# Sliding-window attention with sinks and a two-layer MLP on one core: a new block order, combined score products, and written lists in place of a planner

## The chip, the cores and the metric

The kernel runs on one core of one Trainium2 chip. The metric is the time in device microseconds (us) of one execution; lower is better. A core has TensorE (PE, matmuls), VectorE (DVE), ScalarE (ACT), GpSimd (POOL) and SyncE (SP). Each engine takes its instructions strictly in the order in which they stand in its queue, and waits at an instruction whose semaphores are not yet reached. POOL and SP also issue DMA transfers, from their own queues.

## The reference

```python
# q, k, v: (4 sequences, 8 heads, 768 tokens, 64), float32; n_sink = 4, window = 128
scores = q @ k.T / 8
keep = (key < 4) | ((query - key >= 0) & (query - key < 128))
a = softmax(where(keep, scores, -1e9))
x = (a @ v) as (3072 tokens, 512)
h = x @ w_in                                   # (512, 2048)
out = (h / (1 + exp(-1.702 * h))) @ w_out      # (2048, 512)
```

Attention has a window of 128 tokens and four sink keys, so a block of 128 queries needs the keys and values of its own block, of the block before it in its sequence (masked to the complementary triangle), and four sink keys. The first block of a sequence needs only itself.

## The kernel before

The 3072 tokens are 24 blocks of 128, six to a sequence: blocks 0, 6, 12 and 18 are first blocks. Two neighbouring blocks make a group (12 groups) for the two-layer product.

For one block the steps are these. Three loads, q, k and v, are issued on POOL (L316, L312), which cast from float32 to float16; they are 128 KB each at the destination. q and k are transposed into `qkT`, for the early blocks by TensorE (L410) with a copy out of PSUM, for the others by a DMA transpose on SP (L429). TensorE makes the scores of eight heads against the own block (`own`) and against the previous block (`prv`), eight matmuls of 128 columns with 64 rows each (L460), and the sinks' scores (`snk`, L483). VectorE merges: `prv` is copied over `own` where the key position lies later than the query (L501), the row maximum follows (L513, L529, L532) and is subtracted into `e` (L568, L583). ScalarE takes the exponential into `a` (L600); for half of the heads of the first four blocks it reads PSUM directly with the maximum as bias (L554). `a` is transposed into `at`, by TensorE for the first four blocks (L636), by a DMA transpose on SP for the others (L668). On POOL two selects then split the merged block: `atp` keeps the previous block's triangle (L603), `at` the own one (L607). TensorE sums the values (`av`: L687 the sinks, L693 own, L697 previous), VectorE divides (`xn`, L708, L709), and `xn` is transposed into `xT`, by TensorE (L722) or by DMA (L733).

For one group, TensorE makes the hidden rows `hT` in eight units of eight matmuls of 256 columns (L754; group 0 in units of one block), ScalarE applies the gate into `gT` (L784; group 0 by tanh, L768 and L775), and TensorE makes the output `o` in four quarters per block (L800), which is copied and stored. All `hT`, `o` and transposes share three PSUM buffers (`mm`); scores have `own` 2 and `pv` 2 (shared by `prv` and `av`), sinks 1. The exponential and the gate need different function tables on ScalarE; a change is one ACT_TABLE_LOAD. The weights come as eight loads of 512 KB on POOL (L325, L334).

The order is made by a planner (class Plan): each step is an Op with a cost, an engine, dependencies and a key out of the list KEYS; the planner plays them against the clock and emits them, and emission stands under `with tc.manual_schedule()`, so that each engine's queue has exactly that order. Loads of the later blocks are spread by due times (`after0`, `after`).

Of the kernel before, what the change touches and what calls it, by code (L numbers as in the profile page):

```python
# [20 lines left out]
D = 64  # L21
D1 = D + 1
NBLK = 24
NG = 12
NEG = -1.0e30
PE, ACT, DVE, POOL, SP = "PE", "ACT", "DVE", "POOL", "SP"
CFG = dict(
    tq=(0, 1, 2, 3, 4, 5, 6, 7),
    ta=(0, 1, 2, 3),
    tx=(0, 1, 2, 3),  # L30
    nb={0: 1, 1: 1, 2: 1, 3: 1},
    wide=(1, 3),
    split=(0,),
    gbatch={},
    tanh=(0,),
    after0=25.0,
    vsb=15.0,
    after=8.0,
    loads="q0 k0 q1 k1 v0 v1 i0 i1 q2 k2 q3 k3 i2 i3 v2 v3 q4 k4 q5 k5 o0 o1 o2 o3 v4 v5".split(),
)  # L40
RING = dict(qkn=4, qkt=8, e32=4, a16=4, at=4, atp=4, xn=3, xt=4, gt=3, osb=4, mm=3, own=2, pv=2, mi=1, th=2)

KEYS = [
    int(x)
    for x in """
# [33 lines left out]
""".split()  # L81
]
# [3 lines left out]
class Buf:  # L86


    def __init__(self, ring, make):
        self.ring, self.make, self.ap, self.left, self.taken = ring, make, None, 0, False  # L90
# [7 lines left out]
class Op:  # L98
    def __init__(self, eng, key, cost, emit, deps=(), take=(), give=(), table=None, lat=0.2, xfer=0.0, after=0.0, batch=0, xt=False):
        self.eng = eng if isinstance(eng, dict) else {eng: cost}  # L100
        self.key, self.emit = key, emit
        self.deps = [d for d in deps if d is not None]
        self.take, self.give, self.table, self.batch = list(take), list(give), table, batch
        self.lat, self.xfer, self.after, self.xt = lat, xfer, after, xt
        self.on = self.start = None
        self.end = self.done = 1.0e9
        for b in self.give:
            b.left += 1

    def need(self):  # L110
        rings = [b.ring for b in self.take if not b.taken]
        return {r: rings.count(r) for r in rings}


class Plan:
    TABLE, LANES = 1.35, 8
    ENGINES = (PE, ACT, DVE, POOL, SP)

    def __init__(self, rings):
        self.ops, self.free, self.blk = [], dict(rings), 0  # L120

    def add(self, *a, **kw):
        op = Op(*a, **kw)
        op.seq, op.blk = len(self.ops), self.blk
        self.ops.append(op)
        return op

    def run(self):
        inf = 1.0e9
        t_eng = {e: 1.0 for e in self.ENGINES}  # L130
        free, table, batch, now = dict(self.free), "exp", 0, 0.0
        order, gives, events = [], [], [1.0]
        pending = {e: sorted((o for o in self.ops if e in o.eng), key=lambda o: (o.key, o.seq)) for e in self.ENGINES}
        events += [op.after for op in self.ops if op.after > 0.0]
        queue = {POOL: [], SP: []}
        lanes = {POOL: [], SP: []}
        count = len(self.ops)

        def finish(op):
            events.append(op.done)  # L140
            for b in op.give:
                b.left -= 1
                b.t = max(getattr(b, "t", 0.0), op.done)
                if b.left == 0:
                    gives.append((b.t, b.ring))
                    events.append(b.t)

        while count or any(queue.values()):
            for item in [x for x in gives if x[0] <= now]:
                gives.remove(item)  # L150
                free[item[1]] += 1
            for e in self.ENGINES:
                if t_eng[e] > now:
                    continue
                for op in pending[e]:
                    if op.start is not None or op.after > now:
                        continue
                    if batch and op.table is not None and op.table != table:
                        continue
                    if any((d.end + 0.03 if d.on == e and not d.xfer else d.done) > now for d in op.deps):  # L160
                        continue
                    if any(free[r] < n for r, n in op.need().items()):
                        continue
# [6 lines left out]
                if op.table is not None:  # L170
                    if op.table != table:
                        cost, table = cost + self.TABLE, op.table
                    if op.table == "gate":
                        batch = (batch or op.batch) - 1
# [688 lines left out]
```

## Time and profile before

| | |
|---|---|
| time, median of 3 runs | 251.15 us (249.34 to 252.67) |
| span of the profiled execution | 249.6 us, 5368 instructions |
| loads on POOL | 72 of 128 KB, some 0.90 us each to issue; 8 of 512 KB, 0.78 us |
| DMA transposes on SP | at 20 (3.4 us to landing), xT 20 (2.5), qkT 16 (4.2) |
| selects of a whole block on POOL | L603 1.10 us, L607 1.11 us |
| selects of half a block | 0.65 us, 0.64 us |
| table loads on ScalarE | 20, 1.283 us each |
| HBM | read 27.43 MB, written 6.29 MB |

Times are from one profiled execution. Busy times are shares of its span; TensorE's matmuls overlap, so the mean time of one is longer than the step from one to the next, which the chain of waits shows. A line of the chain in order of time gives start, length and what ran or was waited for. A timeline gives start, length, engine, line and operation, and in brackets the idle time before it and what ended it. "SPq" and "POOLq" are the engines' queues.

### The profile page before, as it was taken

The page shows a single profiled execution, that of the slowest core. Times are in us where ns is not written, and L with a number is a line of the kernel's source. Part 1 is how long each engine was busy: PE and PEld are TensorE (multiplying, and loading weights), DVE is VectorE, ACT ScalarE, POOL GpSimd, SP SyncE. Part 2 cuts the span into 40 slices and gives each one's busy share as a digit, 9 for nine tenths or more (in the row PEclk, how much of TensorE's full clock was granted, in tenths as well). Part 3 has the DMA queues.
Part 4 walks back from the last instruction along what each step waited for, and adds up shares of the span by engine and source line. Part 5 has one row for each costly group of instructions (what it writes and reads, how often), then busy time and mean ns, then how long its engine had stood idle before and what let it go on. Part 6 is the DMA issues. An engine that isn't in the chain of part 4 may idle for free.

```text
span 249.6 us, 5368 instructions
## 1 busy us (share of the span) xinstructions
PE 222.8 (89%) x2163; PEld 151.4 (61%) x2163; DVE 137.0 (55%) x337; ACT 133.2 (53%) x201; POOL 115.5 (46%) x131
## 2 busy tenths in 40 slices
PE   1649768999949999999979999999999999999993
PEld 0328666567526658648637658667567577585751
DVE  4377978958704659869743855616828826001000
ACT  2363657274733747547564557565474677461521
POOL 8869845872931529229705908474042070300000
PEclk9999979999997999999999999999999999999999
DMA  8999999999999979999999999979980360511202
GB/s 64 150 172 181 182 187 197 137 113 167 150 145 231 97 121 185 138 168 153 163 132 243 97 176 193 96 145 188 146 175 11 65 158 3 131 45 21 84 3 84
DMA packets 134440, 33.05 MB, mean 132 GB/s; under 512 B 127216, under 2 KB 131344, under 8 KB 134416
## 3 DMA queue, kind: packets, MB, share of 16 engines
q0 software_dynamic: 79104, 13.64, 77.4%
q1 hardware_dynamic: 55312, 19.08, 41.2%
q8 instruction: 17, 0.28, 0.5%
q14 instruction: 7, 0.06, 0.1%
HBM read 27.43 MB, written 6.29 MB: 135 GB/s over the span
## 4 chain that ended last, share of the span: by engine, by line
PE 69%; DMA 11%; DVE 8%; POOL 7%; issue 3%; ACT 1%; ACTq 0%; POOLq 0%
PE hT L754 31%; PE o L800 26%; DMA xT<-xn 7%; DMA v<-in_v_dram 4%; POOL qkn L316 3%; PE own L460 3%; PE prv L460 2%; PE av L693 2%; PE av L697 2%; POOL at L607 1%; POOL atp L603 1%; DVE mx L513 1%; PE av L687 1%; POOL v L312 1%; DVE gT L775 1%
## 5 line engine op out<-in xcount | busy, mean ns | idle before, releaser
L754 PE MATMUL hT<-xT,w_in 128*128 128x256 f16 (+1 forms) x832 | 93.7, 269 | 7.7 <-DMA xT<-xn 5.9
L800 PE MATMUL o<-w_out,gT 128*128 128x512 f16 x384 | 91.4, 381 | 0.0
L754 PEld LDWEIGHTS <-w_in 128*128 128x128 f16 x832 | 76.3, 100 | 21.2 <-DMA xT<-xn 6.2
L784 ACT ACTIVATE gT<-hT 128x512 f16<-128x512 f32 x88 | 51.7, 597 | 40.1 <-PE hT L754 39.8
L603 POOL TENSOR_SCALAR_AFFINE_SELECT atp<-at 128x1024 f16<-128x1024 f16 (+1 forms) x23 | 22.5, 978 | 92.7 <-DMA at<-a 89.6
L800 PEld LDWEIGHTS <-gT 128*128 128x128 f16 x384 | 34.8, 98 | 35.3 <-issue 0.7
L501 DVE COPY_PREDICATED own<-later,prv 128x512 f32<-128x512 uint16 x40 | 26.1, 695 | 50.6 <-PE prv L460 45.0
L600 ACT ACTIVATE a<-e 128x1056 f16<-128x1056 f32 (+3 forms) x27 | 24.3, 915 | 21.2 <-issue 15.2
L513 DVE TENSOR_REDUCE mx<-own 128x4 f32<-128x512 f32 x48 | 31.7, 683 | 5.0 <-PE own L460 5.0
L568 DVE TENSOR_TENSOR e<-own,mx 128x512 f32<-128x512 f32 x44 | 29.6, 684 | 1.5 <-DVE mx L532 0.5
L389 ACT COPY osb<-o 128x512 f32<-128x512 f32 x20 | 11.7, 586 | 25.1 <-PE o L800 21.3
L607 POOL TENSOR_SCALAR_AFFINE_SELECT at<-at 128x1024 f16<-128x1024 f16 (+1 forms) x23 | 22.8, 990 | 1.6
L316 POOL DMA_DIRECT2D qkn<-in_k_dram x24 | 21.7, 908 | 3.6 <-DMA w_out<-in_moe_w_out_dram 2.5
L316 POOL DMA_DIRECT2D qkn<-in_q_dram x24 | 21.6, 901 | 2.4 <-DMA w_in<-in_moe_w_in_dram 2.2
L312 POOL DMA_DIRECT2D v<-in_v_dram x24 | 21.7, 907 | 1.9 <-DMA w_in<-in_moe_w_in_dram 1.2
L709 DVE TENSOR_TENSOR xn<-av,rcp 128x256 f16<-128x256 f32 x48 | 20.4, 424 | 1.7
L708 DVE RECIPROCAL rcp<-av 128x4 f32<-128x4 f32 x48 | 8.4, 175 | 20.7 <-PE av L697 19.2
L693 PE MATMUL av<-v,at 128*128 128x65 f16 x192 | 17.5, 196 | 1.0 <-POOL at L607 0.6
L693 PEld LDWEIGHTS <-at 128*128 128x128 f16 x192 | 14.8, 99 | 5.3 <-POOL at L607 1.4
L460 PEld LDWEIGHTS <-qkT 64*128 64x128 f16 x352 | 10.9, 99 | 9.5 <-issue 7.9
L697 PE MATMUL av<-v,atp 128*128 128x65 f16 x160 | 15.0, 193 | 0.0
L410 PE MATMUL tq<-ident,qkn 128*128 128x128 f16 x64 | 7.6, 261 | 7.9 <-DMA qkn<-in_k_dram 5.2
(48 smaller groups left out, 162.6 us busy)
## 6 DMA issues: line engine op xcount, KB each, us to landing
out_dram<-osb SPq DMA_DIRECT2D x24, 256.0 KB, 2.4
qkn<-in_k_dram POOLq DMA_DIRECT2D x24, 128.0 KB, 7.1
qkn<-in_q_dram POOLq DMA_DIRECT2D x24, 128.0 KB, 6.2
v<-in_v_dram POOLq DMA_DIRECT2D x24, 128.0 KB, 7.2
w_in<-in_moe_w_in_dram POOLq DMA_DIRECT2D x4, 512.0 KB, 9.2
w_out<-in_moe_w_out_dram POOLq DMA_DIRECT2D x4, 512.0 KB, 12.0
at<-a SPq DMA_TRANSPOSE x20, 3.4
xT<-xn SPq DMA_TRANSPOSE x20, 2.5
```

The costliest lines, as they stand in the source:

```text
L312: return sw(key, 0.88, lambda: nc.gpsimd.dma_start(v65[:, b, :, 0:D], src), 0.85, deps=[z_1], after=after)
L316: key, 0.88, lambda: nc.gpsimd.dma_start(buf()[:, i, w], src), 0.87,
L501: nc.vector.copy_predicated(out=own[l](), mask=later.unsqueeze(1).to_broadcast((P, 4, P)), data=prv[l]())
L513: lambda l=l, own=own, small=small: nc.vector.tensor_reduce(out=small[:, l], in_=own[l](), axis=AX.X, op=ALU.max),
L568: nc.vector.tensor_tensor(out=e32()[:, 512 * l : 512 * l + 512].rearrange("p (j s) -> p j s", j=4), in0=own[l](), in1=small[:, l].unsqueez ...
L600: nc.scalar.activation(out=a16()[:, lo:hi], in_=e32()[:, lo:hi], func=AF.Exp, scale=scale)
L603: nc.gpsimd.affine_select(out=atp()[:, lo : lo + n], in_=at()[:, lo : lo + n], pattern=[[0, n], [-1, P]], compare_op=ALU.is_gt, fill=0.0, ...
L607: nc.gpsimd.affine_select(out=at()[:, lo : lo + n], in_=at()[:, lo : lo + n], pattern=[[0, n], [1, P]], compare_op=ALU.is_ge, fill=0.0, ba ...
L693: nc.tensor.matmul(av()[:, j], at()[:, c], v65[:, b, h], start=(r == 0), stop=(r == 0))
L754: nc.tensor.matmul(ht()[:, n], w_in16[:, c, bass.ts(f, P)], xt[g]()[:, c, tok], start=(c == 0), stop=(c == 3))
L784: lambda fs=fs, tok=tok, gt=gt, ht=ht: nc.scalar.activation(out=gt()[:, fs[0] : fs[-1] + 1, tok], in_=ht(), func=AF.Gelu_apprx_sigmoid),
L800: nc.tensor.matmul(po(), gt()[:, F, bass.ts(t, P)], w_out16[:, F], start=(F == 0), stop=(F == NF - 1))
```

## The change

The steps of the computation stay, with these differences.

- Blocks run in the order 0, 6, 12, 18, then 1 to 5, 7 to 11, 13 to 17, 19 to 23. Groups are [0], [6], [12, 18], and then two blocks each in that order: [1, 2], [3, 4], [5, 7] and so on.
- `qkT` is one tile of 14 slots, so that the keys of a block and of the one before it can be addressed together by a step. Eight matmuls of 256 columns make both key blocks' scores; the result holds own and previous columns side by side in `sc` (two halves of heads, two PSUM banks each). The merge copies one side over the other.
- The four first blocks read PSUM for all heads in the exponential. Sinks are copied out of PSUM before use, and share one PSUM buffer (`av`, 1) with the values. `mm` stays at three.
- TensorE transposes q and k, and x, for the first eight blocks of the order, and `a` for the first six; the later q/k and x transposes are DMA transposes of two blocks at once.
- A block's loads depend, in the list, on the last select of the block five places earlier.
- The planner and KEYS are gone; ORDER lists the operations, and `Plan.emit` follows it. The emission does not stand under `tc.manual_schedule()`.

```diff
+BLOCKS = [0, 6, 12, 18] + [6 * s + r for s in range(4) for r in range(1, 6)]
+SLOT = {b: (b // 6 if b % 6 == 0 else 4 + 5 * (b // 6 % 2) + b % 6 - 1) for b in range(NBLK)}
+GROUPS = [[0], [6]] + [[12, 18]] + [BLOCKS[n : n + 2] for n in range(4, 24, 2)]
-RING = dict(qkn=4, qkt=8, e32=4, a16=4, at=4, atp=4, xn=3, xt=4, gt=3, osb=4, mm=3, own=2, pv=2, mi=1, th=2)
+RING = dict(qkn=4, qkn2=3, e32=3, a16=4, at=4, atp=3, ss=3, xn=3, xt=4, gt1=2, gt2=2, osb=4, mm=3, sc=2, av=1, th=2)
...
+    def emit(self, order):
+        letter = {"d": DVE, "a": ACT, "p": POOL}
+        seen = set()
+        for word in order.split():
+            choice = letter.get(word[-1])
+            op = self.ops[int(word[:-1] if choice else word)]
+            assert all(d.seq in seen for d in op.deps), op.name
+            seen.add(op.seq)
+            op.emit(choice) if len(op.eng) > 1 else op.emit()
...
+                            nc.tensor.matmul(
+                                t()[:, l, jj], qkT[rows, s, j], qkT[rows, lo : hi + 1 : hi - lo, 4 + j],
+                                start=True, stop=True,
+                            )
...
+                    nc.vector.copy_predicated(
+                        out=t()[:, :, :, own].rearrange("p l j s -> p (l j) s"),
+                        mask=later.unsqueeze(1).to_broadcast((P, 4, P)),
+                        data=t()[:, :, :, 1 - own].rearrange("p l j s -> p (l j) s"),
+                    )
...
+            o = plan.add(f"snk{b}", PE, 0.16, sinks, deps=o_qkt[b] + [o_ks[bb]], take=[snk], key=K0 - 32)
...
+    for pos, b in enumerate(BLOCKS):
+        if pos - AHEAD >= 0 and last_sel.get(BLOCKS[pos - AHEAD]):
+            for w in "qkv":
+                ld[w, b].deps.append(last_sel[BLOCKS[pos - AHEAD]])
...
-    order = plan.run()
-    with tc.manual_schedule():
-        for op in order:
-            op.emit(op.on) if len(op.eng) > 1 else op.emit()
+    plan.emit(ORDER)
```

The dependencies given to `plan.add` are not waits of the program: `emit` only asserts that the list respects them. The waits of the program come from the tiles that an instruction reads and writes.

The list and the built program differ. This is POOL's queue from the start, with the selects named by their block (sp makes `atp`, so makes `at`; halves in the first two blocks) and the number of loads between them:

```
list:   35 loads | sp1 sp1 so1 so1 | 3 | sp2 so2 sp2 so2 | 2 | sp3 | 1 | so3 | 3 | sp4 so4 | 3 | sp5 so5 | 3 | sp7 so7 | ...
built:  48 loads | sp1 sp1 so1 so1 | 7 | sp2 | 1 | so2 | 1 | sp2 | 1 | so2 | 1 | sp3 | 1 | so3 sp4 | 1 | so4 | 10 | sp5 | 1 | so5 | 8 | sp7 so7 sp9 so9 ...
```

Both have eight weight loads among the first. In the built program the 51st load waits, beside its place among the loads in flight, for the DMA transpose of blocks 7 and 8, whose buffer it overwrites. SP's queue in the built program has the DMA transposes in the order qkT of 5, of 7 and 8, of 11, of 9 and 10, at of 3, of 4, qkT of 13 and 14, of 15 and 16, of 17, at of 5, of 7, of 9, xT of 5 and 7, with stores between them. In TensorE's queue av of block 1 stands within the first product of [12, 18], av of block 2 within the second product of [12, 18], av of block 5 between two quarters of the second product of [1, 2], after the first unit of [3, 4], and av of block 7 between quarters of the second product of [3, 4]. ScalarE's queue has 44 table loads (in the list 42).

More of the change, by code (lines that the diff above doesn't have):

```diff
@@ L98, with __init__ @@
 class Op:
-    def __init__(self, eng, key, cost, emit, deps=(), take=(), give=(), table=None, lat=0.2, xfer=0.0, after=0.0, batch=0, xt=False):
+    def __init__(self, name, eng, cost, emit, deps=(), take=(), give=(), table=None, dma=None, key=0.0):
+        self.name, self.emit, self.table, self.dma, self.key = name, emit, table, dma, key
         self.eng = eng if isinstance(eng, dict) else {eng: cost}
-        self.key, self.emit = key, emit
         self.deps = [d for d in deps if d is not None]
[L103 to L108, printed above, removed]
@@ L110, in need, with __init__ @@
-    def need(self):
-        rings = [b.ring for b in self.take if not b.taken]
-        return {r: rings.count(r) for r in rings}
+        self.take, self.give = list(take), list(give)
 class Plan:
[L116 to L120, printed above, removed]
+    def __init__(self):
+        self.ops = []
     def add(self, *a, **kw):
         op = Op(*a, **kw)
-        op.seq, op.blk = len(self.ops), self.blk
+        op.seq = len(self.ops)
@@ new lines, with vs_build @@
+    o_vsb = []
+    for bb in range(Bsz):
+        o = plan.add(
+            f"vsa{bb}", SP, 0.75, lambda bb=bb: nc.sync.dma_start(vsa[:, bb, 0:D], v[bb, :, 0:4, :]),
+            deps=[z_s], dma=("c", 0.3), key=-500 + bb,
+        )
+        def vs_build(e, bb=bb):
+            (nc.vector if e == DVE else nc.gpsimd).tensor_tensor(
+                out=vsb[:, bb].rearrange("p l (j d) -> p (l j) d", d=D1),
+                in0=vsa[:, bb].unsqueeze(1).to_broadcast((32, 8, D1)),
+                in1=ownm.rearrange("p (n d) -> p n d", d=D1),
+                op=ALU.mult,
+            )
+        o_vsb.append(plan.add(f"vsb{bb}", {DVE: 0.6, POOL: 1.15}, 0, vs_build, deps=[o, o_own], key=20))
@@ new lines, with head @@
+    o_qkt, o_ks, o_x = {}, {}, {}
+    xts, used_a16, used_slot, last_sel = {}, {}, {}, {}
+    for grp in GROUPS:
+        t = sb("xt", (P, max(map(len, GROUPS)), 4, P), FP16, f"xT{grp[0]}")
+        for n, b in enumerate(grp):
+            xts[b] = (t, n)
+    def head(i):
+        return 2 * (2 * (i // 4) + i % 2) + i // 2 % 2
+    for pos, b in enumerate(BLOCKS):
+        bb, r = divmod(b, 6)
+        K0 = 10 * pos
+        early = pos < COLD
+        lo, hi = sorted((SLOT[b], SLOT[b - 1])) if r else (0, 0)
+        own = int(r == 0 or SLOT[b] > SLOT[b - 1])
+        qkb = qkT[:, SLOT[b]]
+        buf, n, unit = tunit[b]
+        if b in TQ:
@@ L414 @@
                 a = plan.add(
[L415 to L416 removed]
+                    f"t{'qk'[w]}{b}", PE, 0.43 if early else 0.24, t_qk, deps=[ld["qk"[w], b], o_ident],
+                    take=[tp], give=[buf], key=K0 - 40,
                 )
@@ L439, in sink_keys @@
                     nc.vector.tensor_copy(
-                        out=ksb[rows, bb, :, 4 * hl : 4 * hl + 4], in_=qkt[b]()[rows, 4:8, 0:4]
+                        out=ksb[rows, bb, :, 4 * hl : 4 * hl + 4], in_=qkb[rows, 4:8, 0:4]
                     )
-            o_ks[bb] = plan.add(DVE, K0 - 40, 0.7, sink_keys, deps=o_qkt[b] + [z_k])
-        own = [ps("mm" if b in CFG["wide"] else "own", (P, 4, P), FP32, f"own{b}_{l}") for l in range(2)]
-        prv = [ps("pv", (P, 4, P), FP32, f"prv{b}_{l}") for l in range(2)]
@@ L508 @@
-        mx = []
-        for l in range(2):
-            mx.append(
-                plan.add(
-                    DVE, K0 - 38.9, 0.6,
-                    lambda l=l, own=own, small=small: nc.vector.tensor_reduce(
-                        out=small[:, l], in_=own[l](), axis=AX.X, op=ALU.max
-                    ),
-                    deps=[packs[l]],
+            o_ks[bb] = plan.add(f"ks{b}", DVE, 0.35, sink_keys, deps=o_qkt[b] + [z_k], key=K0 - 10)
+        e32 = sb("e32", (P, 8 * P + 32), FP32, f"e32_{b}")
@@ new lines, in exp @@
+        def exp(lo, hi, a16=a16, e32=e32):
+            nc.scalar.activation(out=a16()[:, lo:hi], in_=e32()[:, lo:hi], func=AF.Exp, scale=scale)
+        halves = b in TA
+        e_snk = None
+        if halves or NB.get(b):
+            for hf in range(2):
+                if exps[hf] is None:
+                    o = subs.pop(0)
+                    exps[hf] = plan.add(
+                        f"ex{b}_{hf}", ACT, 0.5, lambda hf=hf, f=exp: f(512 * hf, 512 * hf + 512),
+                        deps=[o] + zero, give=[e32], table="exp", key=K0 - 28,
+                    )
+            if r > 0:
+                e_snk = plan.add(
+                    f"exs{b}", ACT, 0.13, lambda f=exp: f(1024, 1056), deps=[o_ss] + zero,
+                    give=[e32], table="exp", key=K0 - 28,
+                )
+        else:
+            w = 1056 if r > 0 else 1024
+            e = plan.add(
+                f"ex{b}", ACT, 0.93 if r else 0.9, lambda w=w, f=exp: f(0, w),
+                deps=subs + ([o_ss] if r else []) + zero, give=[e32], table="exp", key=K0 - 28,
+            )
+            exps = [e, e]
```

806 lines of the change are left out of this document (359 added, 447 removed), and 33 rows, old and new, of the table KEYS.

## The prediction

> **What bounds the kernel now.** I read the page first: busy shares and slices, then the chain.
>
> ```profile
> PE 222.8 (89%) x2163; PEld 151.4 (61%) x2163; DVE 137.0 (55%) x337; ACT 133.2 (53%) x201; POOL 115.5 (46%) x131
> ...
> PE   1649768999949999999979999999999999999993
> ...
> DMA  8999999999999979999999999979980360511202
> ...
> PE 69%; DMA 11%; DVE 8%; POOL 7%; issue 3%; ACT 1%; ACTq 0%; POOLq 0%
> ```
>
> TensorE is the bound, and almost alone from 80 us on: the stretches give it 156.9 busy of the 160 us from 80 to 240. Its idle time lies at the start (11.0 us in the first 20), between 20 and 60 (5.4) and at 70 to 80 (3.2). In the chain, in order of time, the last of these is a hidden-state wait:
>
> ```profile
> 67.03 6.93 DMA xT<-xn
> ```
>
> So what the change can win or lose lies before 80 us and in how full TensorE stays later. There the POOL queue decides, in its timeline of the first 40 us:
>
> ```profile
> 10.90 0.85 POOL L325 DMA_DIRECT2D w_in<-in_moe_w_in_dram  x1
> 13.96 0.89 POOL L316 DMA_DIRECT2D qkn<-in_q_dram  x1 [2.20 <-DMA w_in<-in_moe_w_in_dram]
> ...
> 20.77 0.67 POOL L603 TENSOR_SCALAR_AFFINE_SELECT atp<-at 128x512 f16<-128x512 f16 x1
> 21.51 0.64 POOL L607 TENSOR_SCALAR_AFFINE_SELECT at<-at 128x512 f16<-128x512 f16 x1
> ...
> 37.71 0.90 POOL L312 DMA_DIRECT2D v<-in_v_dram  x1
> ```
>
> A load costs POOL 0.9 us, and at 13.96 the thirteenth waits until the fifth (the first w_in) has landed: eight loads may be in flight, then POOL itself stands. Selects are on the same queue, so a select behind loads waits for their landings. The load at 37.71 is the 32nd transfer (24 of q, k, v and 8 of weights); asked for its landing, the trace says:
>
> ```profile
> DMA to landing us min/median/max: 11.2/11.2/11.2
> ```
>
> It lands at 48.9. Its neighbours land 0.86 us apart (46.32, 47.02, 47.86, 48.91): undisturbed, that is the pace. Between 66.7 and 78.5 eight landings take 11.8 us, 1.47 each: three to four DMA transposes were in flight, so they add to the loads, some 1.9 us for one block's qkT or at ((11.8 - 6.9) over about 2.6 such).
>
> The Trainium skill ("DMA: Bandwidth & Descriptors", on issuing engines not being separate DMA queues) says that transfers issued from different engines run on the same 16 DMA engines and interleave. The 1.47 against 0.86 us agrees; it speaks against loading early beside transposes.
>
> **The change, part by part.** *The order.* The list is what the emission follows, but the wrapper that kept the written order (manual_schedule) is gone, and in the built program each queue stands in another order than the list. On POOL the difference is large: the list has 35 transfers ahead of block 1's selects, then three to four loads for each block's selects. Built: 48 transfers; block 1's four selects; 7 loads; block 2's four with 3 loads between them; 1 load; the selects of 3 and 4 (two each) with 2 loads; 10 loads; 5's two selects with 1 load between; the last 8 loads; the selects of 7; then only selects. So the loads are not held by the selects: the selects are held by the loads. Of all parts this alone is on the path.
>
> Its clock, from the rows: the first 32 transfers are the same mix as before, so the 32nd lands at 48.9; the 40th 8 x 0.86 later, with block 5's qkT transposed beside it (1.9), at 57.7. The 48th may be issued then: 58.6. Block 1's selects, 4 x 0.65: 61.2. (Before, block 1's were done at 24.4.) Two loads: 63.0. The next overwrites the buffer of blocks 7 and 8, whose DMA transpose starts at 57.7 behind eight loads; the nearest row is the qkT issued at 71.15, 7.7 us to landing: 65.4. Five loads 4.5, block 2 with its loads 5.3, one load and blocks 3, 4 with theirs 7.1: 82.3.
>
> In the TensorE order av1 stands inside the first product of blocks 12 and 18, av2 inside their second, av5 inside 1/2's second product: each holds what is behind it. So h of blocks 1, 2 starts about 77 (so2 75.2, norm, transpose), TensorE reaches av5 at about 93 (two products of 7 us, 2.5 us of attention) and waits.
>
> Block 5's at comes by a DMA transpose that stands on SP behind the qkT transposes of 13/14, 15/16 and 17. Block 17's are transfers 63 and 64, issued by 85.0; they land at 88.7 by the shortest landing (3.7), or at 98 if loads and transposes add (48.9 + 32 x 0.86 + 22 for about 11.5 block transposes). I take 94, nearer the additive row. Then two issues of 1.3, landing 3.4 (5 contended), select, load, select (3.1): block 5's selects end at 102 [97 to 106; 92 if the hold at 63 is nothing either].
>
> From there TensorE still has 10.3 us ahead of av7 (two quarter products 1.7, seven of h 6.1, scores, av 0.35 each, one more quarter), 2.7 to av7's second half, 0.6 norm, then blocks 5 and 7's x transpose, 2.5 to 7 to land: 18 in all. Block 7's selects (102 + 8 x 0.9 + 2.2 = 111.4) arrive before av7 needs them. The products of the eight last pairs begin at T5 = 102 + 18 = 120.
>
> After T5 TensorE has eight pairs: 8 x (8 x 0.875 + 8 x 0.8625) = 111.2 by the chain's h and o pieces; 22 score halves; 11 sink products 2.0; 28 av halves at 0.35 = 9.8. Before had about 123 us left at 120 (245.5 less some 2.5 of later waits).
>
> *Scores.* 160 products of 128x128 go and the rest are 256 wide. Before: 0.33 us for eight, twice per block, 0.66. Eight of 256 columns: at best the row pairs run side by side, 4 x 0.109 (an h product of 256 columns) = 0.44; at worst one after the other, 0.87. The row 0.33 for eight of 128, where alone a 128 column product of h takes 0.056, is 0.74 of serial, so the middle: 0.5. After T5: 22 x 0.25 = 5.5, bounds 4.8 and 9.6. Over all 20 blocks -3.2 [-4.4, +4.2].
>
> *First blocks first.* Four blocks need no previous block and no select. First h at about 19 instead of 22.4 (the first w_in is the 12th transfer: 11 loads at 0.9 to 1.2 and 2.5 after 3.9, near 18); the last w_out is the 23rd, nine loads ahead of the 32nd, about 41 (before 45.3). A gain of some 4 us of TensorE time by 45 us, eaten by the wait at av1; nothing of it remains in the sum.
>
> *ScalarE.* The table loads rise from 20 to 44, because exps stand singly among the gates: 24 x 1.283 = 31 us more, 164 of about 257. On the path only where h waits for its three buffers: one exp between gates is 1.28 + 1.08 + 1.28 = 3.6 us, and the order puts av, scores and quarters of o (3.1 to 4 us) there. I take 2.7 us of waits in all, before's rate after 80 us; without that cover 1 us for each of about 14 late exps, 14 us.
>
> ```profile
> 157.03 0.60 ACT L784 ACTIVATE gT<-hT 128x512 f16<-128x512 f32 x1 [0.28 <-PE hT L754]
> 157.65 1.28 ACT L600 ACT_TABLE_LOAD   x1
> 158.94 1.08 ACT L600 ACTIVATE a<-e 128x1056 f16<-128x1056 f32 x1
> ```
>
> Nothing stands between gate, load and exp but 0.02 us. The Trainium skill ("ScalarE: Activation LUTs", What ACT_TABLE_LOAD costs) adds a drain of about 1.38 us to each load; the trace does not show it. By that rule ScalarE would be at 107.6 + 44 x 2.66 = 225 us, an estimate from that page, still under the span.
>
> *The rest.* VectorE gains 20 small maxima (0.24) and 16 sink copies (0.19), loses four subtractions (0.68) and a memset (1.8): +3 us at 55%, hidden. Sinks and av share one PSUM buffer instead of three with the previous scores: an av then waits for the norm before it (0.6), which an h or o quarter (0.87) between them hides; bare, 0.6 each. Fewer, double-sized DMA transposes move the same bytes.
>
> **Sum.** T5 120 + 111.2 + 5.5 + 2.0 + 9.8 + waits 2.7 + end 4.1 (last product at 245.5, span 249.6) = 255.3. The median of the runs, 251.15, is 1.5 above the profiled span: 256.8. Two per cent, about what a measurement of this kernel can tell from no change, is 246.1 to 256.2.
>
> **Rivals.** *The forecast* (0.55): 250 to 262, for block 5's selects between 95 and 107. It would be seen as POOL waiting on landings and TensorE idle at av1, av2 and av5.
> *Transfers do not add* (0.25): the DMA transposes slip between the loads. For: from 104.8 to 107.1 loads land 0.78 us apart with a qkT in flight; against: 1.47. Then POOL's own issue time paces it: no wait at 63, block 17 landed by 86, block 5's selects at 90 to 92, T5 108 to 110, time 245 to 247: faster by 2 to 2.5%. It decides below 91 us for those selects.
> *ScalarE uncovered* (0.12): the forecast plus 11 us more waits, 268. For: 3.6 us holes against three buffers; against: the page shows ScalarE's gates waiting 39.8 us for TensorE, so it has slack.
> *The change does what it says, the lists rule in effect* (0.08): selects of 1 behind 35 transfers, done by 47, and 5's by 70. TensorE is then full from about 45: some 209 us of work in all (o 83, h 84, av 16, scores 11, sinks 4, transposes and masks 11), less 25 done by 45 (the products of 6 and 0, 14, and attention), plus 45, 4 end, 5 waits, 1.5: 240. Against: the built order itself.
>
> **Chances.** Faster by over 2%: the list's 0.08 and half of the second, 0.2 in all. Slower by over 2%: 0.3 of the forecast (its own range is 250 to 262; serial scores, +4, lean that way), ScalarE's 0.12 and a little beyond, 0.45. Within: 0.35. The likeliest time is 257. The range takes in the second case with the scores at their best (243) and the forecast's end with them serial (266): left out are the list and most of ScalarE's.
>
> **What would show it.** Right: POOL's 48 issues end at 55 to 60, block 1's selects near 60; TensorE slices near 0 to 5 between 47 and 75 and again around 95 to 120, full after; 44 table loads without idle TensorE beside them; a score group of four at 0.25. Wrong: TensorE full from 50 us, block 5's selects before 91, or idle TensorE after 120 with its h waiting for gates.

## The result, and the profile after

| | before | changed |
|---|---|---|
| time, median | 251.37 us (4 runs) | 285.36 us (4 runs, 281.3 to 286.64) |
| ratio, 95% interval | 1 | 1.127 [1.113, 1.141] |
| span of the profiled execution | 249.6 us | 279.6 us |
| h of the last eight pairs starts (T5) | 112.9 | 132.1 |
| from T5 to the start of the last product o | 132.3 | 143.3 |

The change is 12.7% slower; the forecast was 256.8, called 257, in a range of 243 to 266. All ratios, and the times in the table of the experiments, leave out executions over 1.5% slower than the fastest of their kernel, so that the changed kernel counts there with 282.8 and e1 with 261.5, where the texts written before a run quote 285.4 and 264.5. From the page of the changed kernel: busy time of each engine, TensorE's slices and granted clock, and the chain's shares.

```profile
PE 235.8 (84%) x2042; PEld 148.1 (53%) x2042; DVE 148.6 (53%) x385; ACT 161.0 (58%) x229; POOL 113.2 (40%) x128
...
PE   2398599987298951999999989989899999699994
...
PEclk9997979999779995899999999999999999999998
...
PE 51%; DMA 16%; ACT 11%; DVE 7%; POOL 7%; issue 4%; SPq 3%; ACTq 0%; POOLq 0%; DVEq 0%
```

A slice is 7 us. TensorE is mostly idle in the 11th, half idle in the 15th and nearly all idle in the 16th (70 to 77 and 98 to 112 us), with a lower granted clock in the 11th and 16th, and is not quite full after T5. ScalarE's share of the chain went from 1% to 11%, TensorE's fell from 69% to 51%. The stretches of 10 us show the two holes (columns: busy time and count for PE, PEld, DVE, ACT and POOL, then granted clock, DMA share, GB/s):

```profile
70.00:80.00 10.00, 4.79 (x23) 2.07 (x24) 0.90 (x3) 0.65 (x2) 8.95 (x12) 0.66 2.42 166
...
100.00:110.00 10.00, 1.96 (x13) 0.98 (x10) 0.29 (x1) 1.30 (x2) 2.11 (x3) 0.69 1.51 139
```

The Trainium skill ("TensorE: Matmul & The Clock Gate", Why this matters for your kernels) says that TensorE left idle for more than some 3 us falls back to half its clock. The 0.66 and 0.69 in the two holes fit that; TensorE is idle there anyway, so the holes and not the clock are to be explained. The chain of waits leads through both:

```profile
55.20 12.91 DMA qkT<-qkn
...
74.50 0.67 POOL at L553
75.21 0.24 PE av L626
...
76.92 5.96 DMA at<-a
82.94 1.08 POOL atp L553
...
90.66 5.12 DMA qkn<-in_k_dram
95.92 1.37 SPq L341
97.39 10.37 DMA at<-a
```

The waits of the whole run put TensorE's part and POOL's beside it (engine and line, what it waited for: total, times, longest):

```profile
PE av L626 <- POOL at L553: 10.3, 3, 6.4
...
PE av L621 <- DMA at<-a: 6.2, 1, 6.2
```

```profile
POOL qkn L259 <- DMA qkT<-qkn: 7.6, 1, 7.6
```

The first hole is the forecast one: POOL's 51st load stands 7.6 us for the transpose of blocks 7 and 8, block 2's selects stand behind it, and TensorE waits 6.4 us for them until 75.21. The second hole ends otherwise: block 5's transpose of weights (`at<-a`) is issued at 97.39 and lands 10.37 us later, and TensorE waits 6.2 us for it and 2.8 for the selects behind it. In between, POOL stood 4.0 us until block 3's weights had landed (76.92 + 5.96); the loads of block 17, which block 5's transpose has to wait for in SyncE's queue, stand behind those selects. When could the transposes of weights have started? ScalarE's timeline has the exponentials of blocks 3, 4 and 5 (the first row's second one is block 3's):

```profile
66.04 1.60 ACT L522 ACTIVATE a<-e 128x512 f16<-128x512 f32 x2
68.98 1.08 ACT L522 ACTIVATE a<-e 128x1056 f16<-128x1056 f32 x1 [0.66 <-DVE e L512]
89.29 1.08 ACT L522 ACTIVATE a<-e 128x1056 f16<-128x1056 f32 x1
```

and this is SyncE's own queue (L341 transposes q and k, L597 weights):

```profile
62.38 14.43 SPq L341 DMA_TRANSPOSE qkT<-qkn  x2
76.92 4.67 SPq L597 DMA_TRANSPOSE at<-a  x2
...
91.60 5.69 SPq L341 DMA_TRANSPOSE qkT<-qkn  x2
97.39 7.39 SPq L597 DMA_TRANSPOSE at<-a  x2
```

Block 3's weights were ready at 67.6 and their transpose was issued at 76.92: 9.3 us behind the qkT transpose of 9 and 10, issued at 72.80 once its loads had landed. Block 4's waited 8.6 us, with block 3's. Block 5's were ready at 90.4 and issued at 97.39, 7.0 us later, behind those of 15 to 17. After T5 the chain runs over ScalarE between gates (load of the table, exponential, load, gate), and over an av half whose sinks' product (L621) takes 0.21 and whose end comes 0.56 after its start:

```profile
213.04 1.28 ACT L522
214.34 1.08 ACT a L522
215.44 1.28 ACT L732
216.73 0.61 ACT gT L732
...
229.93 0.21 PE av L621
230.14 0.14 PE av L626
230.49 1.75 PE hT L702 x16
```

### The profile page after: what moved, and what is told of

It is laid out like the page before. It is cut to its first block, busy times and chain, and to the rows that moved or that the text cites. A ratio compares the mean times of both kernels' runs of the same rounds, so it can differ in the third digit from the quotient of the medians.

```text
span 279.6 us, 5141 instructions
## 1 busy us (share of the span) xinstructions
PE 235.8 (84%) x2042; PEld 148.1 (53%) x2042; DVE 148.6 (53%) x385; ACT 161.0 (58%) x229; POOL 113.2 (40%) x128
## 4 chain that ended last, share of the span: by engine, by line
PE 51%; DMA 16%; ACT 11%; DVE 7%; POOL 7%; issue 4%; SPq 3%; ACTq 0%; POOLq 0%; DVEq 0%
PE o L748 21%; PE hT L702 20%; DMA at<-a 7%; DMA qkT<-qkn 5%; ACT L732 3%; PE sc L398 3%; POOL qkn L259 2%; PE av L626 2%; ACT a L522 2%; ACT L522 2%; DMA qkn<-in_k_dram 2%; POOL atp L553 2%; ACT gT L732 2%; DMA vsa<-in_v_dram 2%; POOL at L553 1%
## 5 line engine op out<-in xcount | busy, mean ns | idle before, releaser
L702 PE MATMUL hT<-xT,w_in 128*128 128x256 f16 (+1 forms) x832 | 96.0, 268 | 3.3 <-ACT xT L232 1.5
L748 PE MATMUL o<-w_out,gT 128*128 128x512 f16 x384 | 94.7, 389 | 3.0 <-ACT gT L732 3.0
L702 PEld LDWEIGHTS <-w_in 128*128 128x128 f16 x832 | 75.1, 99 | 16.7 <-issue 7.0
L461 DVE TENSOR_REDUCE mx<-sc 128x4 f32<-128x512 f32 x48 | 32.6, 686 | 5.9 <-PE sc L393 5.3
L451 DVE COPY_PREDICATED sc<-later,sc 128x512 f32<-128x512 uint16 x40 | 27.3, 689 | 13.3 <-PE sc L398 13.1
L232 ACT COPY osb<-o 128x512 f32<-128x512 f32 x16 | 9.3, 584 | 34.9 <-PE o L748 34.9
L498 DVE TENSOR_TENSOR e<-sc,mx 128x512 f32<-128x512 f32 x40 | 26.8, 685 | 0.6
L522 ACT ACTIVATE a<-e 128x1056 f16<-128x1056 f32 (+2 forms) x24 | 22.2, 935 | 3.3 <-DVE e L512 1.8
L626 PEld LDWEIGHTS <-at 128*128 128x128 f16 x192 | 13.1, 102 | 16.8 <-POOL at L553 11.2
L621 PE MATMUL av<-vsb,at 32*128 32x260 f16 x40 | 11.4, 285 | 8.2 <-DMA at<-a 6.2
```

Source lines behind the costliest of these rows:

```text
L451: nc.vector.copy_predicated(out=t()[:, :, :, own].rearrange("p l j s -> p (l j) s"), mask=later.unsqueeze(1).to_broadcast((P, 4, P)), data ...
L461: nc.vector.tensor_reduce(out=part, in_=t()[:, :, :, own], axis=AX.X, op=ALU.max)
L498: nc.vector.tensor_tensor(out=e32()[:, 512 * hf : 512 * hf + 512].rearrange("p (l j s) -> p l j s", l=2, j=2), in0=t()[:, :, :, own], in1= ...
L522: nc.scalar.activation(out=a16()[:, lo:hi], in_=e32()[:, lo:hi], func=AF.Exp, scale=scale)
L626: nc.tensor.matmul(av()[:, i], at()[:, c], v65[:, b, h], start=(r == 0), stop=(r == 0))
L702: nc.tensor.matmul(ht()[:, n].rearrange("p (n t) -> p n t", n=NT), w_in16[:, c, bass.ts(f, P)], t0()[:, i0 : i0 + NT, c], start=(c == 0), ...
```

## The experiments

Ratios are to the kernel before on the same chip (its medians there were 249.6 to 250.5), with 95% intervals. T5 and the rest (T5 to the last product o) are from the profiled execution, which took 263.6 us in e10 and 247.3 in e15. "As built" is the changed kernel's order, taken operation by operation; "list" is ORDER, kept by `tc.manual_schedule()`.

| run | PE, DVE, ACT | POOL's loads | SP | besides | us | ratio | T5 | rest |
|---|---|---|---|---|---|---|---|---|
| e1_list | list | list | list | | 261.5 | 1.045 [1.035, 1.056] | 113.4 | 144.0 |
| e2_list_early | list | built | built | | 282.8 | 1.132 [1.124, 1.140] | 137.8 | 138.9 |
| e3_built_held | built | list | list | | 278.5 | 1.115 [1.107, 1.123] | 116.9 | 154.6 |
| e4_built_manual | built | built | built | | 298.1 | 1.189 [1.183, 1.195] | 138.8 | 153.9 |
| e5_list_tanh | list | list | list | no table loads | 258.7 | 1.033 [1.016, 1.050] | 110.6 | 143.3 |
| e6_list_single | list | list | list | single qkT | 257.2 | 1.028 [1.008, 1.048] | 111.1 | 141.3 |
| e7_early_single | list | built | built | single qkT | 279.7 | 1.118 [1.100, 1.135] | 136.2 | 138.5 |
| e8_early_ring4 | list | built | built | 4 buffers, by the pool | 280.3 | 1.120 [1.106, 1.133] | 134.5 | 139.0 |
| e9_early_nohold | list | built | built | 4 buffers, in turn | 280.7 | 1.121 [1.107, 1.134] | 135.9 | 139.1 |
| e10_early_pool_list_sp | list | built | **list** | 4 buffers, in turn | 262.3 | 1.043 [1.030, 1.056] | 119.3 | 138.4 |
| e11_list_sinks128 | list | list | list | sinks 128 rows | 259.3 | 1.035 [1.023, 1.047] | 112.2 | 141.2 |
| e12_list_mended | list | list | list | both, exps moved | 270.2 | 1.078 [1.071, 1.084] | 107.9 | 155.9 |
| e13_built_sp_list | built | built | **list** | 4 buffers, in turn | 274.5 | 1.097 [1.087, 1.106] | 114.6 | 152.8 |
| e14_list_single_rows | list | list | list | single qkT, sinks 128 | 251.6 | 1.004 [0.998, 1.010] | 107.6 | 137.2 |
| e15_list_all_tanh | list | list | list | e14, no table loads | 244.7 | 0.978 [0.969, 0.987] | 105.5 | 135.8 |
| e16_early_pool_mended | list | built | list | e10 with e14's two | 257.1 | 1.027 [1.021, 1.033] | 116.4 | 133.8 |
| e17_tanh_mid_groups | list | list | list | e14, gates 5 to 9 on DVE | 271.9 | 1.086 [1.080, 1.092] | 107.5 | 158.0 |
| e18_changed_sinks128 | as changed | as changed | as changed | sinks 128 rows | 281.5 | 1.124 [1.116, 1.132] | 133.6 | 140.2 |

**The order: list or built.** e1 puts the wrapper back. e2 to e4 are the same operations under it, with ORDER rewritten so that some queues stand as built.

```diff
-    plan.emit(ORDER)
+    with tc.manual_schedule():
+        plan.emit(ORDER)
```

> The changed kernel with the emission under the wrapper that keeps the written order, so that every queue is the list: 35 loads ahead of block 1's selects, 42 table loads instead of 44. Theory A (the built order's early loads hold the selects and stretch the first 130 us): block 1's selects end near 50 us, block 5's before 80 instead of 110.9, no 10 us stretch between 60 and 130 with TensorE under 8 us busy, time 240 to 255. Theory B (the order of TensorE, VectorE and ScalarE is what costs): the same sign, since the list undoes both; the two next kernels part them. Rival C (the steps themselves, 42 table loads and the shared buffers, are the cost, whatever the order): 270 or more.

> The list for TensorE, VectorE and ScalarE, but POOL's and SP's queues in the order in which they were built (48 loads ahead of block 1's selects). Theory A: within 5 us of the changed kernel's 281 to 285, block 5's selects end at 105 to 115 us. Theory B: within 5 us of the list kernel.

> TensorE, VectorE and ScalarE in the built order (44 table loads), POOL and SP in the list's order. Theory A: block 5's selects before 85 us and a time 20 us or more under the changed kernel's, that is 250 to 262. Theory B: 272 to 285.

> All five queues in the built order, step by step (the built program also cuts into steps here and there, this one does not), under the wrapper. All theories: 278 to 287, as the changed kernel; if it is far off, the cutting into steps matters and the comparison of the others must be made against this one.

The list takes off about 21 us of the changed kernel's loss, not the 45 of my rival; it stands 4.5% over the kernel before, between e1's theories. e2 came out as its theory A and e3 as its theory B. The two parts nearly add: POOL's and SyncE's queues as built cost 21 us with the list's engines (e1 to e2) and 20 with the built ones (e3 to e4), the other three engines' order 17 and 15. e4 came out above its 278 to 287, some 5.5% slower than the changed kernel (1.189 against 1.127), which has this order cut into single instructions. So the list kernels do not repeat the changed kernel exactly, and what follows is shown for them.

**Which of POOL and SyncE?** Both were moved together in e2. I first suspected what the chain showed at 55.20: a transpose of two blocks, 12.9 us to landing, with a load behind it on POOL. e7 issues each transpose of two blocks as two, e8 adds a buffer.

```diff
-                nc.sync.dma_start_transpose(
-                    qkT[:, s : s + len(unit)].rearrange("p r c t -> p (r c) t"),
-                    buf()[:, 0 : len(unit)].rearrange("p n w h d -> p (n w h d)"),
-                )
+                for x in range(len(unit)):
+                    nc.sync.dma_start_transpose(qkT[:, s + x], buf()[:, x].rearrange("p w h d -> p (w h d)"))
```

> The list's order for TensorE, VectorE and ScalarE with the loads as early as the changed kernel has them (as e2_list_early, 282.8 us, last pairs' h at 137.8), and each transpose of two blocks issued as two of one block. Theory A (the size of the transpose made 12.9 us of what I had put at 7.7, and POOL stood at the load behind it): the transposes of blocks 7 and 8 land 4 to 6 us sooner, h of the last pairs starts at 130-134, the time is 275-279. Theory B (the traffic of the early loads makes any transpose late): T5 stays at 136-139, the time at 281-285.

> As e2_list_early (282.8 us, last pairs' h at 137.8) with a fourth buffer for the q and k of two blocks, so that POOL's load of block 15 no longer waits for the transpose of blocks 7 and 8 (7.6 us in the changed kernel). Theory A (that hold of POOL stands on the path to block 5's selects): T5 falls by 6-8 us to 130-132, the time to 275-277. Theory B (the selects are bound by what the transposes of the weights take beside the loads, and the loads only start earlier): T5 135-138, the time 280-284.

Both miss theory A. In e7 single transposes of blocks 5, 7 and 8 took 8.9 to 9.3 us to landing as well, each with five to seven loads in flight when it was issued; so the size is not what made them late. e8 gained little, and did not do what I meant: POOL's load of block 13 still waited 6.99 us for the transpose of 7 and 8. e9 writes the rotation out:

```diff
+    qk2s = [const.tile([P, 2, 2, H, D], FP16, name=f"qk2_{i}") for i in range(4)]
...
+            buf = Buf(None, lambda i=pairs.index(unit) % 4: qk2s[i])
```

> As e8_early_ring4 (280.3 us, last pairs' h at 134.5), with the four buffers for q and k of two blocks written out and taken in turn: in e8 POOL's load of block 13 still stood 6.99 us at the transpose of blocks 7 and 8, since it had been given their buffer. Theory A (that stand delays the selects of blocks 2 to 5): h of the last pairs starts 6-7 us sooner, at 127-129, the time is 273-275. Theory B (the selects wait for transposes of the weights, which stand in SyncE's queue behind those of q and k): T5 133-136, the time 279-282.

> As e9_early_nohold, with SyncE's queue in the list's order (the transposes of the weights of blocks 3, 4, 5 ahead of those of q and k of 9, 13, 15 and 17), POOL's loads as early as in the changed kernel. Theory B (SyncE's order: in the changed kernel the weights of block 3 stood ready at 67.6 and those of block 5 at 90.4, but their transposes were issued at 76.9 and 97.4, behind transposes of q and k that wait for loads and for TensorE): T5 at 115-121, the time 261-267, as e1_list (264.5). Theory A (POOL's order and the traffic): T5 at 126-129, the time 272-275.

The wait went and the time stayed (280.7): theory A falls. The products of blocks 1 and 2 did start 4.4 us sooner than in e2 (79.4 for 83.8), but T5 fell by 1.9 only. e10 then changes SyncE's order alone, and takes 18 us away:

```
as built: qkT5 qkT7,8 [2 stores] qkT11 qkT9,10 at3 at4 [store] qkT13,14 [store] qkT15,16 qkT17 at5 at7
list:     [2 stores] qkT5 at3 at4 [2 stores] qkT7,8 at5 qkT9,10 at7 [2 stores] qkT11 xT7 at9
```

SyncE's queue in e10 (L602 weights, L346 q and k), and ScalarE's exponential of block 5:

```profile
65.56 6.61 SPq L602 DMA_TRANSPOSE at<-a  x2
...
75.32 3.43 SPq L346 DMA_TRANSPOSE qkT<-qk  x1
81.41 1.94 SPq L602 DMA_TRANSPOSE at<-a  x1
```

```profile
80.25 1.08 ACT L527 ACTIVATE a<-e 128x1056 f16<-128x1056 f32 x1
```

Block 5's transpose is issued at 81.41, 0.1 us after its exponential ends (80.25 + 1.08), where the changed kernel took 7.0; it lands 7.6 us later, for 10.4. TensorE's waits at av (engine and line, what it waited for: total, times, longest) were in e2

```profile
PE av L626 <- POOL at L553: 17.5, 4, 11.4
PE av L621 <- DMA at<-a: 7.3, 2, 5.9
```

and in e10 (its lines stand five further down) the first and the fourth of the list:

```profile
PE av L631 <- DMA qk<-in_q_dram: 5.3, 1, 5.3
...
PE av L631 <- POOL at L558: 3.6, 4, 1.3
```

POOL has the same order in e9 and e10, loads ahead of selects. In e9 TensorE waited 5.7 us at av of block 2, for selects behind loads that stood for others still in flight, and twice for weights of blocks 3 and 5 (9.5 us); in e10 block 2's wait is 1.2 us and no wait for weights is left. So POOL's order alone does not make the 18 us: SyncE's does, where transposes that wait for late loads stand ahead of transposes whose data are ready, and run beside POOL's loads. POOL's order keeps a smaller part: the 5.3 us in e10 are for block 7's selects, again behind loads, and T5 is 119.3 where the list has 113.4. e13 asks the same with the built order of the three engines (two operations of block 13 were moved by a few places, as in e3, or the queues would block each other).

> TensorE, VectorE, ScalarE and POOL in the order that the changed kernel was built with, operation by operation (e4_built_manual: 298.1 us, last pairs' h at 138.8), SyncE's queue in the list's order, and the four buffers for q and k of two blocks taken in turn. Theory B (SyncE's order carries the slip): T5 at 118-122, the time 277-282, as e3_built_held, where POOL's loads were held too (278.5). Rival (POOL's early loads and the engines' own order carry it here): T5 at 132-138, the time 290-297.

T5 goes from 138.8 to 114.6 and the time from 298.1 to 274.5, earlier and faster than theory B had it. e3, with the same order on the other four queues but POOL's loads held, is not faster (116.9, 278.5). e13 also has e9's buffers, which took 1.9 us off T5 there. In the changed kernel itself SyncE's order could not be set apart, since no list gives its order of single instructions; that it carries most of its 19 us to T5 (132.1 against e1's 113.4) too is read from the 9.3, 8.6 and 7.0 us above, and not shown by a run.

**What is left in the list.** e1 still loses 4.5%. Three runs take one suspect each (e6's edit is e7's).

> The list's own order on every queue (as e1_list, 264.5 us, start of the last pairs' products h at 113.4, 144.0 us from there to the last product o), with every gate as tanh(0.851 x), which shares the exponential's table: the gate's multiplication by x is left out, so the output is another function, and some 39 of ScalarE's 41 table loads go. Theory A (ScalarE's swaps between gates and exponentials set the pace of the last groups): 41 loads x 1.28 us are 52 us of ScalarE, of which some 12 us stood on the path after 113; the rest after h of the last pairs falls from 144 to 132-134 and the time to 250-254. Theory B (TensorE's own order, the one av buffer, transposes that land late): the rest stays at 141-144, the time at 261-265.

> The list's order (e1_list, 264.5 us), with each transpose of q and k of two blocks issued as two transposes of one block from the same buffer, at the same place of SyncE's queue. Theory A (the transposes of two blocks land late, 10.9 us at 72 and 7.7 at 185 where a single one took 4.2 in the kernel before, and TensorE waits): each pair lands 3 to 5 us sooner, the last pairs start at 108-111 instead of 113.4, the time is 257-261. Theory B (they are hidden, or it is the wait for the loads and not the size): 262-266, and two issues of some 1.2 us each in place of one delay the transposes of the weights behind them.

> The list's order (e1_list, 264.5 us), with the product of the sinks' values over 128 rows as in the kernel before (the rows beyond 32 of its second operand are zero) instead of over 32. Theory A (a product of 260 columns starts its successor after 212 ns where 32 rows are given and after 110 where 128 are): 40 x 0.102 = 4.1 us less on TensorE, 28 of them behind the start of the last pairs: the time 259.5-262, the rest after T5 141 instead of 144. Theory B (TensorE has that time to spare): 263-266.

The edit of e11, whose second operand is zero beyond row 32:

```diff
-    vsb = const.tile([32, 4, 2, 4 * D1], FP16, name="vsb")
+    vsb = const.tile([P, 4, 2, 4 * D1], FP16, name="vsb")
...
-                        av().rearrange("p j d -> p (j d)"), at()[0:32, 8], vsb[:, bb, hf], start=True, stop=False
+                        av().rearrange("p j d -> p (j d)"), at()[:, 8], vsb[:, bb, hf], start=True, stop=False
```

Each comes out 1 to 1.7 points of the ratio under e1, with intervals that overlap e1's: alone, none is settled. e12 joined two of them with a third, and missed by far:

```diff
 ScalarE:
-ex14 g7_0 g7_2 ev9 g7_6 g7_1 g7_3 g7_4 ex15 g7_5 g7_7 ex16
+ex14 g7_0 g7_2 ev9 g7_6 g7_1 g7_3 g7_4 g7_5 g7_7 ex15 ex16
```

> The list's order with three things mended: transposes of q and k of one block each (e6_list_single: 257.8), the sinks' product over 128 rows, and the exponentials of blocks 10, 13, 15, 17 and 20 moved behind the gates in whose midst they stand, next to the following block's (10 of ScalarE's 41 table loads go). Theory A (the three add up): 257.8 - 4.1 - 2 to 4 = 249.5-252, level with the kernel before. Theory B (what is taken off one engine waits for another, and the moved exponentials hold their selects): 255-259.

(`ex` is a block's exponential, `g` a gate, `ev` the copy of an output.) Its T5 is the earliest till then, 107.9, and its rest 155.9. TensorE's waits from 112 to 240 us are for what follows an exponential:

```profile
PE hT L700 <- DMA xT<-xn: 8.6, 3, 6.6
PE av L624 <- POOL at L551: 5.5, 3, 2.1
```

and, 3.7 us, for transposes of weights. An exponential among the gates costs two table loads, but one to four gates later its weights, selects and x come too late for TensorE: e14, which is e12 with the exponentials left where they were, is 18.5 us faster. e15 takes the loads away instead.

> The list's order with transposes of q and k of one block each and the sinks' product over 128 rows. If the two costs add (6.6 and 4.4 us off 264.5): 253-255, 1.01 of the kernel before. If the one is hidden beside the other: 257-260.

> As e14_list_single_rows with every gate as tanh(0.851 x), its multiplication by x left out, so that ScalarE's table loads go. If the three costs make up what the list loses against the kernel before: 246-250. If ScalarE's loads only filled waits for the other two: 252-255.

```diff
-                        out=gt()[:, fs[0] : fs[-1] + 1], in_=ht(), func=AF.Gelu_apprx_sigmoid
+                        out=gt()[:, fs[0] : fs[-1] + 1], in_=ht(), func=AF.Tanh, scale=0.851
```

e14 is level with the kernel before (1.004) and below its 253 to 255: the two mends together take 4.1 points off e1's ratio, where each alone took 1.7 and 1.0, within wide intervals. 41 table loads less give another 2.6, and the intervals of e1, e14 and e15 lie apart. The chain of e14 near the same place as the changed kernel's shows the av half's new length:

```profile
220.36 0.11 PE av L619
...
220.69 0.03 PE av L626
220.72 1.75 PE hT L700 x16
```

0.36 from its start to the next product, against 0.56: 40 halves make 8 us of TensorE, of which e14 shows 5.6 in its time against e6, the same kernel with 32 rows. The Trainium skill ("TensorE: Matmul & The Clock Gate", Why this matters for your kernels) says that a single matmul over 32 rows takes the same time as one over 128. Its own length agrees (mean 285 ns in the changed kernel, 274 before); what stands around it does not: it starts 205 ns after a product of h instead of 109, and its successor starts 212 ns after it instead of 110.

**Early loads with everything mended, a gate on VectorE, and the changed kernel itself.**

> As e10_early_pool_list_sp (262.3 us), with transposes of q and k of one block each and the sinks' product over 128 rows. If the mends add up as with the list's loads: 252-255. If the transposes are late there because of the loads in flight beside them and not for their size: 257-260, the sinks' 4 us alone.

e16 has the shortest rest of the whole gates' kernels (133.8) and a T5 of 116.4; the time (257.1) is that of its second case. Against e14, early loads beside the transposes still cost some 9 us before T5, and return 3.4 after it.

> As e14_list_single_rows (251.6 us), with the gates of groups 5 to 9 in the form that block 0 has: a tanh on ScalarE (the exponential's table) and (1 + tanh) times h on VectorE, the half taken when the output is evicted; the whole gate is computed. 20 of 40 table loads go, 25.7 us of ScalarE; VectorE gets 40 products of 0.6 us, 24 us, and each tile of h is held some 1 us longer in one of three buffers. Theory A (the loads cost): half to all of the 5.8 us that they cost in all: 246-249, faster than both kernels. Theory B (TensorE waits for h's buffers, which VectorE now frees, behind its maxima): 254-260.

```diff
-TANH = {0}
+TANH = {0, 5, 8, 10, 13, 15}
```

(the first block of each group is named, `th` has three buffers, and the list was rewritten for the new operations). Theory B, and worse than it: TensorE's waits from 112 to 240 us are now for VectorE's product (L723).

```profile
PE hT L702 <- DVE gT L723: 8.6, 13, 1.5
PE o L748 <- DVE gT L723: 8.4, 6, 2.6
```

e14 has none of these, and waits 4.1 us in all in that stretch. The loads cost less than either way that I tried to avoid them, so no kernel that computes the whole reference beat the one before: e14 is level with it.

> The changed kernel as it is (285.4 us), with the sinks' product over 128 rows and nothing else. If those 4.1 us are on the path there too: 280-282. If TensorE waits for the selects before the last pairs anyway (12 of the 40 products), only the other 28 count: 281.5-283.5. If it is hidden: 284-287.

281.5 is the edge between the first two cases, but these were counted from 285.4. By the table's count the changed kernel takes 282.8, so the gain is 1.3 us, with intervals that overlap (1.124 [1.116, 1.132], 1.127 [1.113, 1.141]); the rest is 3.1 us shorter, T5 1.5 later. Whether the sinks' 4.1 us are on the path of the changed kernel stays open.

## Why the prediction was wrong

The direction was as forecast, and so were two of the three places where TensorE was to idle, av of block 2 and of block 5; at av of block 1 it waited 0.7 us only, and the slices between 47 and 70 us read 7 to 9, not the 0 to 5 that I named. The time was 28.5 us over the sum. It splits so: T5 132.1 for 120 (+12.1); the rest 143.3 for 131.2 (+12.1); the end 4.2 for 4.1; and the median 5.8 over the profiled span for 1.5 (+4.3; the profiled execution itself took 281.3, 1.7 over its span).

- **"Of all parts this alone is on the path"**, POOL's loads ahead of the selects: the step that failed. In these runs that order is not what carries the slip to T5. With POOL as built and SyncE as listed the last pairs start at 119.3 (e10) and 114.6 (e13); with POOL's loads held too, at 113.4 (e1) and 116.9 (e3). Putting SyncE's order right moves T5 by 16.6 us (e9 to e10) and 24.2 (e4 to e13, with e9's buffers). What was right is the first hole: block 2's selects were done at 78.1 for 75.2. The clock that I built on POOL's order held in its early rows (32nd transfer landed 48.1 for 48.9, 48th issued 55.96 for 58.6, block 1's selects done at 59.3 for 61.2), so it looked sound. The hold at the 51st load was there (7.6 us), and T5 fell by only 1.9 us when it went (e9). I used SyncE's queue for block 5 alone, and not for blocks 3 and 4, whose transposes stood ready for 9.3 and 8.6 us.
- **Block 5's at**: block 17's loads landed at 95.8 for 94 and the transpose was issued at 97.39, near the forecast; then "landing 3.4 (5 contended)" took 10.37 us. That is the mis-sized term in the clock of the 102: selects ended at 110.9. The kernel before had shown single transposes of 7.7 and 9.0 us beside loads; I used its median. From there 21.1 us for 18.
- **The transpose of 7 and 8**: 12.9 us for 7.7; e7 and e9, which shorten it or take the hold away, start the last pairs 1.6 and 1.9 us sooner than e2.
- **Scores 0.25 a half**: 0.32 to 0.33 in the chain, 8.1 us after T5 for 5.5. Pairs of 256 columns do run side by side (successors of a pair stand 106 to 117 ns apart, my lower bound's 109), but each half pays some 0.1 us more on leaving for a product of 128 rows, and as much on entering in most places. Eight narrow products took as long (0.33). Nothing is saved.
- **"28 av halves at 0.35"**: 15.2 us for 9.8, 0.54 each on average. That the sinks' product was cut from 128 rows to 32 I had not costed at all. With h and o 6.6 us over their 111.2, by waits and such steps, and sinks 2.2 for 2.0, the four (6.6, 2.6, 5.4, 0.2) less the 2.7 us of waits that I allowed are the 12.1.
- **"2.7 us of waits in all" with ScalarE covered**: 44 loads came as counted. The uncovered rival gave 11 us more; without its loads e14 is 6.9 us faster (e15). In the changed kernel the loads stand in the chain after T5, but no run took them out there.
- **"The lists rule in effect", 240**: 261.5. Of the 21 us two mends take off 10 and the table loads 7; no run shows where the remaining 5 lie.
- **The first blocks' gain of 4 us**: the first h came at 22.1, as before (22.4); with the list at 19.4. TensorE had made two blocks' h and began the next 2.6 us sooner in the changed kernel (51.1 for 53.7) and 5.8 sooner with the list (47.9).
- **The chances** put most on slower (0.45), but the range stopped at 266, since every rival moved the start of the last pairs or ScalarE, and none both T5 and the rest.

## What to carry to other kernels

When a queue's order changes, list for each entry when its data are ready and when it is issued; an entry that waits for a late load delays all that is ready behind it, and the engine that shows the wait (here POOL) need not be the one whose order causes it. When an operand's shape changes, cost the step to the next instruction and not the instruction's own length. An edit that removes a cost can lose more by where it moves the work: both ways around the table loads (later exponentials, gates on VectorE) lost 18 to 20 us to save at most 7.

## What the runs showed of the hardware

- A product over 32 rows between products over 128 costs TensorE some 0.2 us more than the same one over 128 rows, the added rows zero: an av half 0.56 us (changed kernel) against 0.36 (e14).
- DMA transposes took 2.5 to 4.2 us to landing in the median of the kernel before. With loads in flight single blocks took up to 10.4 us (block 5's weights in the changed kernel; 8.9 to 9.3 for q and k in e7) and two blocks at once 12.9.
- Whole operations in the order as built (e4, 298.1 us) were slower than the changed kernel (282.8), which has that order cut into single instructions; why is not shown.
